# Pooled and banded attention in front of two layers of products: wider fillers, a mask and a sum given to TensorE, and a new plan of the order

## The chip, the cores and the metric

The program runs on one core of one Trainium2 chip. The metric is the device time of one execution in microseconds (us), lower is better; the median over several executions is taken. Beside the times, one profiled execution is recorded, with every instruction of the engines: TensorE (PE, its weight loads apart as PEld), VectorE (DVE), ScalarE (ACT), GpSimd (POOL) and SyncE (SP), which issues nearly all transfers here.

## What is computed

```python
def _attn_ref(q, k, v):                       # B, H, S, D = 4, 8, 576, 64
    q_d, k_d, v_d = means of q, k, v over groups of 4 positions
    out_d = softmax(q_d k_d^T / 8) v_d
    out_up = np.repeat(out_d, 4, axis=2)
    mask = np.abs(pos[:, None] - pos[None, :]) < 4
    out_local = softmax(where(mask, q k^T / 8, -1e9)) v
    return out_up + out_local

def reference(**kwargs):
    x = attn_out.transpose(0, 2, 1, 3).reshape(2304, 512)
    h = x @ w_in;  g = h * sigmoid(h);        x = g @ w_out    # 512 -> 2048 -> 512
    h = x @ w2_in; g = s * relu(h) ** 2 + b;  return g @ w2_out
```

All of it is fp32. The kernel reaches that precision in the layers by splitting each operand into a high and a low part that TensorE takes at full rate (fp32r), and by three matmuls for each product: high times high, low times high, high times low. The products of the attention are plain fp32 matmuls; the trace shows each of these as two records.

## The kernel before, in words

The 2304 tokens are cut into five blocks of 512, 512, 512, 512 and 256 (`blocks`). `mix1(u)` is the first layer for block u: for each of the 16 pieces of the hidden width it makes `hp` (12 matmuls of 512 columns), SiLU on ScalarE (`g`), a high part on ScalarE (`gh`), a low part on VectorE (`gl`), and then 12 matmuls into the four sums `y`. The second layer is computed with fewer products by sums of its operands: `group` makes its hidden values in the banks `ha`, `hb`, `hc` (and `hp` for the last block), `snap` copies a bank to SBUF (the `COPY g<-ha` of L350), `late` does Relu on ScalarE, the square on VectorE and scale and bias on ScalarE, and the result is stored to HBM (`gd<-g`) and read back (`graw<-gd`) for the last products `oa`, `ob`, `oc`.

Block 0 needs the attention of the first batch, and nothing of a layer can start before it. This stretch, up to about 45 us, is made of eight *pieces*: `banded` is called for each pair of heads (four) and each half of the batch's first 512 positions. A piece scores (`pB`, L841), adds the mask of the band on VectorE (`be<-pB,band`, L846), takes the minimum (L867) and the exponentials (L854), turns the result (`pBT`, L882) and copies it (`bat`), multiplies by V (`pBO`, L895) and adds the pooled attention on VectorE (`xf<-pBO,upT`, L904). When all pieces of a head pair are there, `x_split(0)` makes the high part `xh` on ScalarE (L584) and the low part `xl` on VectorE (L585), each 128x512, four times. The rest of the attention is done between the matmuls of the first blocks.

The order is not written by hand. Each operation is given to a planner (`Weave.op`) with its engine, a cost in us, what it reads and writes, and a number `pr`; `Weave.plan` goes through time and always starts what can start first, the lower `pr` first, and `Weave.run` emits the program in that order. Operations marked `EITHER` go to ScalarE or VectorE as the plan finds them free. The tables at the top (`P_...`, `NAT0`, `PB0`, ...) give these numbers and so the order on every engine and in the queue of SP. Where the plan leaves PE idle by over 0.12 us before block 0's split is done, `Weave.run` puts fillers in: matmuls on zeros into a bank that is not read (`spin`), as many of 64 columns as 0.85 of the planned gap holds at 0.03 us each. 100 fillers stand at the program's start (`NWARM`).

The second layer's weights come as 64-bit integers of fp64 bits and are converted once (`whole`, 32 times; `to_f32`): with `ACTW2` a ScalarE operation (L400, `f<-w_raw`) and two on VectorE (L403 and L410), without it three on VectorE (L408, L410, L412). What is converted is stored, and `y_sums`, `w_sums` and `out_sums` later load it again as `wt`, `wb` and `wout`; a `CAST wt<-wt` on ScalarE follows each load of `wt`.

Of the kernel before, what the change touches and what calls it, by code (L numbers as in the profile page):

```python
# [42 lines left out]
NNAT, NVW = 10, 4  # L43
AHEAD = 4
MORE = 0.0
RAW, KEEP = 1.68, 0.82
NEARLY = 0
MASKED = False
ADDED = False
P_IN, P_OUT, P_Y0, P_W0, P_Y1, P_Y4, P_W, P_OS = 163.074, 237.937, 134.047, 31.694, 78.573, -4.134, 81.417, 4.352  # L50
P_STEP, P_BT, P_PO, P_PN = 6.074, -5.7, 16.567, 57.528
P_G, P_B, P_C = 89.387, -1.232, -7.24
D1, D1S = 8, 2
NWARM = 100
ACTW, ACTW2 = 0, True
TANH = 0
# [9 lines left out]

NAT0, NATS = -3.387, 1.422
VW0, VWS, VW1 = 6.355, 0.281, 27.579
RAWF, RAW0, RATE = 35.769, 5.781, 1.255
DECF, DEC0, DECS = 47.826, 49.984, 0.829  # L70
PT0, PTS = 31.757, 3.611
PN0, PNS = 5.815, 6.313
PB0, PBS = -2.568, 16.345
NAT1, PT1, PT1S = 33.957, 58.357, 3.543
LDP = 49.468

# [209 lines left out]
def pe(n):  # L286
    return n / 2400.0 + 0.0145


@with_exitstack  # L290
def kernel(ctx, tc, q, k, v, w1_in, w1_out, w2_in, w2_out, s2, b2, cst, out):
# [82 lines left out]
    op("sp", (1, 0.25), lambda: dma(csb.tile, cst[:, :P]), w=[csb], pr=-100)  # L374
    op("sp", (1, 0.3), lambda: dma(band.tile, cst[:, P + 2 * NM:]), w=[band], pr=-2.9)
    by_chunk = cst[:, P:P + 2 * NM].rearrange("(k c) m -> c k m", k=KD)
# [4 lines left out]
    pad = fixed(cp, [P, 24], F32, "pad")  # L381
    idle = Buf("g", [P, P], BF16, "idle")
    spin = Buf("y3", [P, 64], F32, "spin")
    op("dve", 0.1, lambda: nc.vector.memset(idle[:], 0.0), w=[idle], pr=-200)

    def fill(n):
        for _ in range(n):
            nc.tensor.matmul(spin[:], lhsT=idle[:], rhs=idle[:, :64], start=True, stop=True)

# [36 lines left out]
    def weights(m, pr, after, lpr=None):  # L426
        got = []
        end = mark("end")
        for nm in ("wi", "wo"):
            t = Buf("w", [P, KD, P, 2], I32, nm + "_raw")  # L430

            op("sp", (1, 1.45 if nm == "wi" else 1.27), lambda t=t, nm=nm: load_in(w1_in, m, t[:]) if nm == "wi" else load_out(w1_out, m, t[:]),
               w=[t], r=after, pr=pr if lpr is None else lpr)
            f = Buf("f32", [P, KD, P], I32, "f32")
            o = Buf("w", [P, 2, KD, P], F32R, nm)
            to_f32(t, f, pr, [end], 0.0, m >= ACTW, m < GPS)
            halves(f, o, pr)
            got.append(o)
# [172 lines left out]
    def rows(b, i, names, pr, kind, after=[], by="sp"):  # L611

        for nm in names:
# [10 lines left out]

            op(by, (2, 1.35, 0.45) if nm == "v" else (2, 1.45, 0.5), load, w=[t], r=after, pr=pr)

# [155 lines left out]
    def b_load(b, hqs, js, pr, after=[]):  # L782
# [21 lines left out]
        k = (2 if mid else 0) + len(ends)  # L804
        move = 0.188 * len(js) * len(hqs)
        op(by, (k, move, 0.5), load, w=[vw], r=after, pr=pr)
        return vw

    def banded(b, hqs, js, vw, vi, pr, ps, after=[]):
# [97 lines left out]
        if added:  # L907
            (xh, xl), (e, i), cols = [t[hqs[0] // 2] for t in xs[u]], divmod(hqs[0], 2), slice(col, col + n)
            key = (hqs[0], js[0])
            op(EITHER, (act(n), dve(n)), lambda eng: copy(eng, xh[:, i, cols], pO[:]), w=[(xh, key)], r=[pO], pr=-4)  # L910
            op("dve", dve(n), lambda: nc.vector.tensor_tensor(out=xl[:, i, cols], in0=pO[:], in1=xh[:, i, cols].bitcast(F32), op=ALU.subtract),
               w=[(xl, key), (split[u][0], key)], r=[pO, (xh, key)], pr=-4)
        else:
            op("dve", dve(nb * QB), add, w=keys, r=[pO] + ups, pr=pr)
# [61 lines left out]
    for hq in A:  # L976
        rows(0, hq, "qk", NAT0 + NATS * hq, "nat")
        rows(0, hq, "v", NAT0 + NATS * hq, "nat", by="act" if hq < NACT else "sp")
    vw0 = [v_load(0, [hq], first, VW0 + VWS * hq) for hq in A]
# [443 lines left out]
```

## Time and profile before

| | us |
|---|---|
| median of 3 executions | 861.76 (861.71 to 862.54) |
| the profiled execution | 864.08 |
| its span, first to last instruction | 862.3 |
| PE busy in the span | 852.2 (99%) |
| VectorE busy | 735.2 (85%) |
| ScalarE busy | 509.0 (59%) |
| mean granted clock of TensorE | 0.998 |

The span is the execution without 1.8 us around it. The busy times are shares of the whole span and hide that the engines' loads differ from stretch to stretch; a busy PE includes the fillers. Matmuls overlap, so the time from the start of one to the start of the next tells what one costs, not its own length.

### The profile page before, as it was taken

The page shows a single profiled execution, that of the slowest core. Times are in us where ns is not written, and L with a number is a line of the kernel's source. Part 1 is how long each engine was busy: PE and PEld are TensorE (multiplying, and loading weights), DVE is VectorE, ACT ScalarE, POOL GpSimd, SP SyncE. Part 2 cuts the span into 40 slices and gives each one's busy share as a digit, 9 for nine tenths or more (in the row PEclk, how much of TensorE's full clock was granted, in tenths as well). Part 3 has the DMA queues.
Part 4 walks back from the last instruction along what each step waited for, and adds up shares of the span by engine and source line. Part 5 has one row for each costly group of instructions (what it writes and reads, how often), then busy time and mean ns, then how long its engine had stood idle before and what let it go on. Part 6 is the DMA issues. An engine that isn't in the chain of part 4 may idle for free. (4 is left out here: it accounts for less than half of the span.)

```text
span 862.3 us, 14707 instructions
## 1 busy us (share of the span) xinstructions
PE 852.2 (99%) x5300; PEld 715.3 (83%) x5300; DVE 735.2 (85%) x1364; ACT 509.0 (59%) x1034; POOL 0.2 (0%) x4
## 2 busy tenths in 40 slices
PE   9999999999999999999999999999998999999998
PEld 8878777778778878888889988888887888888887
DVE  7999996999999999987767789777775899888894
ACT  6988797655456742453556556666666665434351
POOL 0000000000000000000000000000000000000000
PEclk9999999999999999999999999999999999999999
DMA  8995421642444220489995246655577856544411
GB/s 204 297 379 157 129 69 40 195 125 70 106 127 118 70 75 32 128 278 304 335 307 162 75 130 218 219 183 178 181 255 246 271 170 211 173 148 129 122 32 43
DMA packets 163058, 144.26 MB, mean 167 GB/s; under 512 B 65452, under 2 KB 127786, under 8 KB 162986
## 3 DMA queue, kind: packets, MB, share of 16 engines
q1 hardware_dynamic: 162578, 142.96, 52.8%
q8 instruction: 42, 0.69, 0.3%
q10 hardware_dynamic: 408, 0.36, 0.1%
q14 instruction: 30, 0.25, 0.1%
HBM read 102.40 MB, written 40.89 MB: 166 GB/s over the span
## 5 line engine op out<-in xcount | busy, mean ns | idle before, releaser
L925 PE MATMUL hp<-xh,wi 128*128 128x512 f32 (+1 forms) x640 | 200.8, 377 | 0.2 <-ACT g L950 0.2
L925 PE MATMUL y<-gh,wo 128*128 128x512 f32 (+1 forms) x640 | 199.8, 376 | 0.0
L925 PEld LDWEIGHTS hp<-xh,wi 128*128 128x128 f32 x640 | 116.9, 188 | 23.1 <-ACT g L950 2.7
L925 PEld LDWEIGHTS y<-gh,wo 128*128 128x128 f32 x640 | 117.0, 189 | 19.9 <-issue 0.8
L925 PE MATMUL y<-gl,wo 128*128 128x512 f32 (+1 forms) x320 | 118.2, 369 | 0.0
L925 PE MATMUL hp<-xl,wi 128*128 128x512 f32 (+1 forms) x320 | 117.9, 369 | 0.0
L925 PE MATMUL ha<-yh,wi 128*128 128x512 f32 x256 | 87.8, 393 | 2.4 <-ACT g L350 2.4
L951 ACT CAST gh<-g 128x512 fp32r<-128x512 f32 (+1 forms) x80 | 46.1, 577 | 53.3 <-PE y L925 52.6
L950 ACT ACTIVATE g<-hp 128x512 f32<-128x512 f32 (+1 forms) x80 | 44.4, 555 | 42.1 <-DVE gl L952 36.9
L1138 ACT ACTIVATE g<-g,sbt 128x512 f32<-128x512 f32 (+1 forms) x72 | 54.7, 766 | 23.5 <-DVE g L1133 23.0
L925 PEld LDWEIGHTS y<-gl,wo 128*128 128x128 f32 x320 | 60.5, 189 | 8.8 <-DVE gl L952 0.3
L925 PEld LDWEIGHTS hp<-xl,wi 128*128 128x128 f32 x320 | 60.5, 189 | 8.2
L952 DVE TENSOR_TENSOR gl<-g,gh 128x512 fp32r<-128x512 f32 (+1 forms) x80 | 50.6, 633 | 17.7 <-ACT gh L951 17.6
L1133 DVE SCALAR_TENSOR_TENSOR g<-g 128x512 f32<-128x512 f32 (+1 forms) x80 | 49.7, 633 | 13.7 <-ACT g L1132 13.2
L925 PEld LDWEIGHTS ha<-yh,wi 128*128 128x128 f32 x256 | 48.4, 189 | 13.2 <-ACT g L350 3.7
L1265 ACT CAST gh<-gs 128x1024 fp32r<-128x1024 f32 x27 | 28.4, 1051 | 44.8 <-DVE gs L1261 37.2
L1265 ACT CAST gh<-graw 128x1024 fp32r<-128x1024 f32 x36 | 37.4, 1050 | 24.6 <-PE ob L1291 9.7
L925 PE MATMUL ha<-yl,wi 128*128 128x512 f32 x128 | 50.2, 393 | 0.0
L1266 DVE TENSOR_TENSOR gl<-graw,gh 128x1024 fp32r<-128x1024 f32 x36 | 43.6, 1218 | 4.9 <-PE oa L1284 4.0
L350 ACT COPY g<-ha 128x512 f32<-128x512 f32 x48 | 28.1, 585 | 31.1 <-PE ha L925 25.1
L925 PE MATMUL hc<-yh,wi 128*128 128x512 f32 x128 | 45.4, 395 | 0.0
L542 DVE TENSOR_TENSOR tmp<-le,lv 128x1344 f32<-128x1344 f32 (+1 forms) x28 | 37.9, 1354 | 0.5
(198 smaller groups left out, 1723.0 us busy)
## 6 DMA issues: line engine op xcount, KB each, us to landing
graw<-gd SPq DMA_DIRECT2D x36, 512.0 KB
gd<-g SPq DMA_DIRECT2D x64, 256.0 KB
wi_raw<-in_moe_w_in_dram SPq DMA_DIRECT2D x16, 512.0 KB
wo_raw<-in_moe_w_out_dram SPq DMA_DIRECT2D x16, 512.0 KB
w_raw<-in_moe_w_in_dram SPq DMA_DIRECT2D x16, 512.0 KB
w_raw<-in_moe_w_out_dram SPq DMA_DIRECT2D x16, 512.0 KB
nq<-in_q_dram SPq DMA_DIRECT2D x32, 144.0 KB
nk<-in_k_dram SPq DMA_DIRECT2D x32, 144.0 KB
```

The source lines that it names most:

```text
L350: (nc.scalar.copy if eng == "act" else nc.vector.tensor_copy)(out=out, in_=in_)
L542: op("dve", dve(n * WIN * D), lambda t=t, i0=i0, n=n, h2=h2: nc.vector.tensor_tensor(out=t[:], in0=wide(e[:, h2 * ns + i0:h2 * ns + i0 + n ...
L925: nc.tensor.matmul(t(), lhsT=lhs(i), rhs=rhs(i), start=(first and i == 0), stop=(last and i == 2), **kw)
L950: op("act", act(n), lambda g=g, hp=hp: nc.scalar.activation(out=g[:], in_=hp[:], func=AF.Silu), w=[g], r=[hp], pr=-5, table="silu")
L951: op("act", act(n), lambda g=g, gh=gh: nc.scalar.copy(out=gh[:], in_=g[:]), w=[gh], r=[g], pr=-5)
L952: op("dve", dve(n), lambda g=g, gh=gh, gl=gl: nc.vector.tensor_tensor(out=gl[:], in0=g[:], in1=gh[:].bitcast(F32), op=ALU.subtract), w=[gl ...
L1133: op("dve", dve(n) + 1.5 * MORE, lambda: nc.vector.scalar_tensor_tensor(out=t[:], in0=t[:], scalar=0.0, in1=t[:], op0=ALU.max, op1=ALU.mul ...
L1138: nc.scalar.activation(out=t[:], in_=t[:], func=AF.Identity, scale=sbt[:, 0:1], bias=sbt[:, 1:2])
L1265: op("act", act(HF * P) + MORE, lambda: nc.scalar.copy(out=flat(hi), in_=flat(x)), w=[hi], r=[x], pr=pr + n)
L1266: op("dve", dve(HF * P) + MORE, lambda: nc.vector.tensor_tensor(out=flat(lo), in0=flat(x), in1=flat(hi).bitcast(F32), op=ALU.subtract), w= ...
```

## The change

Fillers: `fill` makes one filler of 256 columns of every four of 64; the 100 at the start stay. `MASKED`: in the eight pieces of the first batch the mask is added by TensorE, as a product of the identity and the band into the same bank (`pB<-band,csb`, L837 after); the VectorE addition is gone, and minimum and exponentials read the bank. `ADDED`: the pooled attention is added in the same way (`pBO<-upT,csb`, L892 after, one of 256 columns for each piece), and `xh` and `xl` are made from the bank, piece by piece, 128x256 each. `ACTW2` is off. `AHEAD` (how many pieces of the first layer's weights may be loaded ahead of their conversion) goes from 4 to 3. The planner's costs for a few loads change, among them the longer blocks of keys of V, and all tables of numbers are new. All lines below the table move down by one or two.

```diff
-AHEAD = 4
+AHEAD = 3
-MASKED = False
-ADDED = False
-P_IN, P_OUT, P_Y0, P_W0, P_Y1, P_Y4, P_W, P_OS = 163.074, 237.937, 134.047, 31.694, 78.573, -4.134, 81.417, 4.352
+MASKED = True
+ADDED = True
+P_IN, P_OUT, P_Y0, P_W0, P_Y1, P_Y4, P_W, P_OS = 122.797, 178.953, 66.766, 19.092, 141.386, -9.23, 157.685, 125.641
...
-ACTW, ACTW2 = 0, True
+ACTW, ACTW2 = 0, False
...
-    return n / 2400.0 + 0.0145
+    return n / 2400.0 + 0.0143
...
-    idle = Buf("g", [P, P], BF16, "idle")
-    spin = Buf("y3", [P, 64], F32, "spin")
+    idle = Buf("g", [P, 4 * 64], BF16, "idle")
+    spin = Buf("y3", [P, 4 * 64], F32, "spin")
...
     def fill(n):
-        for _ in range(n):
-            nc.tensor.matmul(spin[:], lhsT=idle[:], rhs=idle[:, :64], start=True, stop=True)
+        wide, n = divmod(n, 4) if n < NWARM else (0, n)
+        for k in [4] * wide + [1] * n:
+            nc.tensor.matmul(spin[:, :64 * k], lhsT=idle[:, :P], rhs=idle[:, :64 * k], start=True, stop=True)
...
-            op(by, (2, 1.35, 0.45) if nm == "v" else (2, 1.45, 0.5), load, w=[t], r=after, pr=pr)
+            op(by, (2, 1.15, 0.45) if nm == "v" else (2, 1.27, 0.5), load, w=[t], r=after, pr=pr)
...
-        move = 0.188 * len(js) * len(hqs)
+        move = (0.25 if b == 0 and len(hqs) == 1 else 0.188) * len(js) * len(hqs)
...
-            (xh, xl), (e, i), cols = [t[hqs[0] // 2] for t in xs[u]], divmod(hqs[0], 2), slice(col, col + n)
+            (xh, xl), half, cols = [t[hqs[0] // 2] for t in xs[u]], hqs[0] % 2, slice(col, col + n)
...
-    for hq in A:
-        rows(0, hq, "qk", NAT0 + NATS * hq, "nat")
-        rows(0, hq, "v", NAT0 + NATS * hq, "nat", by="act" if hq < NACT else "sp")
+    for hq in A:
+        for nm in "qkv":
+            rows(0, hq, nm, NAT0 + NATS * hq + (PV if nm == "v" else 0.0), "nat", by="act" if nm == "v" and hq < NACT else "sp")
```

What `MASKED` and `ADDED` switch stands in `banded`, `x_split` and `parts` above, in the branches on `early` and `added`.

**First place.** PE at the first score of the first batch: `spin` are fillers, `pq` turns q and k of a head pair, `pB` is a piece's bank. Before:

```order
L388 LDWEIGHTS idle
L388 MATMUL spin<-idle 128x64
L841 MATMUL pB<-qkT 64x72 x16
L702 MATMUL pS<-dk,q_diag_87 96x144 x3
L774 MATMUL pq<-csb,nq 128x96 x6
```

After:

```order
L837 MATMUL pB<-band,csb 128x72
L837 MATMUL pB<-band,csb 128x216
L843 MATMUL pB<-qkT 64x72 x8
L837 MATMUL pB<-band,csb 128x288
L843 MATMUL pB<-qkT 64x72 x8
L704 MATMUL pS<-dk,q_diag_87 96x144 x3
L776 MATMUL pq<-csb,nq 128x96 x3
L776 MATMUL pq<-csb,nk 128x96 x6
L776 MATMUL pq<-csb,nq 128x96 x3
L390 LDWEIGHTS idle
L390 MATMUL spin<-idle 128x256
```

The two pieces of a head pair, 16 scores in one row before, stand together in both. The first now begins with two products of the mask (72 and 216 columns) and the second with one (288 columns); the fillers are cut into pieces of 256 columns. Over the whole program the order of PE has 368 fillers before; after, 100 at the start, 15 of 256 columns and 9 of 64. The new products are 12 of the mask and 8 of the pooled sum. The times that PE goes from other work into the layers' products are 92 before and 88 after.

**Second place.** ScalarE ahead of the copy for which PE waits near 662 us, a copy of bank `ha` (`g_7582` before, `g_7348` after), from the last cast of `wt`. Before:

```order
L350 CAST wt_7457<-wt_7457 128x512
L1132 ACTIVATE g_7502<-ha 128x512
L1138 ACTIVATE g_7484<-g_7484,sbt 128x256
L1132 ACTIVATE g_7528<-hp_7504 128x256
L1138 ACTIVATE g_7502<-g_7502,sbt 128x512
L1138 ACTIVATE g_7443<-g_7443,sbt 128x512
L1138 ACTIVATE g_7528<-g_7528,sbt 128x256
L1132 ACTIVATE g_7553<-hp_7524 128x256
L1138 ACTIVATE g_7553<-g_7553,sbt 128x256
L1132 ACTIVATE g_7568<-hp_7544 128x256
L1138 ACTIVATE g_7568<-g_7568,sbt 128x256
L350 COPY g_7582<-ha 128x512
```

After:

```order
L351 CAST wt_7223<-wt_7223 128x512
L1134 ACTIVATE g_7275<-hp_7225 128x256
L1140 ACTIVATE g_7253<-g_7253,sbt 128x512
L1134 ACTIVATE g_7293<-hp_7267 128x256
L1140 ACTIVATE g_7275<-g_7275,sbt 128x256
L1134 ACTIVATE g_7311<-hp_7287 128x256
L1140 ACTIVATE g_7205<-g_7205,sbt 128x512
L1140 ACTIVATE g_7293<-g_7293,sbt 128x256
L1140 ACTIVATE g_7311<-g_7311,sbt 128x256
L1134 ACTIVATE g_7334<-hp_7307 128x256
L1140 ACTIVATE g_7334<-g_7334,sbt 128x256
L351 COPY g_7348<-ha 128x512
```

Ten operations stand between the last cast and the copy in both, three of 512 columns before and two after. Before, the last four are Relu (L1132), scale (L1138), Relu, scale, each scale directly behind its own Relu, with the square of the same values on VectorE (L1133) between them; after, only the last pair stands so.

**Third place.** The queue of SP that feeds these casts: `wt` are the loads, `gd<-g` stores of hidden values, `w2t` stores of sums. Before:

```order
L363 DMA wt_7387<-w2t_92 128x512
L363 DMA wt_7394<-w2t_92 128x512
L363 DMA gd_95<-g_7367 128x512
L363 DMA wt_7419<-w2t_92 128x512
L363 DMA wt_7422<-w2t_92 128x512
L363 DMA gd_94<-g_7398 128x512
L363 DMA wt_7436<-w2t_92 128x512
L363 DMA wt_7445<-w2t_92 128x512
L363 DMA wt_7457<-w2t_92 128x512
L363 DMA gd_95<-g_7338 128x512
L363 DMA gd_94<-g_7380 128x512
```

After:

```order
L364 DMA wt_7153<-w2t_92 128x512
L364 DMA wt_7158<-w2t_92 128x512
L364 DMA w2t_93<-f_7027 128x512
L364 DMA gd_95<-g_7137 128x512
L364 DMA gd_94<-g_7165 128x512
L364 DMA wt_7188<-w2t_92 128x512
L364 DMA wt_7192<-w2t_92 128x512
L364 DMA gd_95<-g_7109 128x512
L364 DMA wt_7212<-w2t_92 128x512
L364 DMA wt_7217<-w2t_92 128x512
L364 DMA wt_7223<-w2t_92 128x512
L364 DMA gd_94<-g_7151 128x512
```

The eighth load of `wt`, an early one, is not among these rows. Before, the last three loads have the store of `gd_94<-g_7398` ahead of them and that of `gd_95<-g_7338` behind; after, both stores (`gd_94<-g_7165` and `gd_95<-g_7109`) are ahead of the last three loads, and the first of them ahead of the two loads before these as well.

**Fourth place.** VectorE at the start of the conversion of the second layer's weights (`w_raw`). Before:

```order
L567 TENSOR_TENSOR xf<-pt,upT 128x4x32 x2
L550 TENSOR_TENSOR tmp<-tmp 128x2x192
L952 TENSOR_TENSOR gl<-g,gh 128x512
L550 TENSOR_TENSOR tmp<-tmp 128x2x128
L403 TENSOR_SCALAR f_4540<-f_4540 128x512
L550 TENSOR_TENSOR pv<-tmp 128x2x64
L410 SCALAR_TENSOR_TENSOR f_4540<-w_raw,f_4540 128x512
L403 TENSOR_SCALAR f_4564<-f_4564 128x512
L403 TENSOR_SCALAR f_4578<-f_4578 128x512
L410 SCALAR_TENSOR_TENSOR f_4564<-w_raw,f_4564 128x512
L410 SCALAR_TENSOR_TENSOR f_4578<-w_raw,f_4578 128x512
```

After:

```order
L410 SCALAR_TENSOR_TENSOR f_4280<-w_raw,f_4280 128x512
L412 SCALAR_TENSOR_TENSOR f_4280<-w_raw,f_4280 128x512
L408 TENSOR_SCALAR f_4300<-w_raw 128x512
L410 SCALAR_TENSOR_TENSOR f_4300<-w_raw,f_4300 128x512
L408 TENSOR_SCALAR f_4311<-w_raw 128x512
L412 SCALAR_TENSOR_TENSOR f_4300<-w_raw,f_4300 128x512
L410 SCALAR_TENSOR_TENSOR f_4311<-w_raw,f_4311 128x512
L412 SCALAR_TENSOR_TENSOR f_4311<-w_raw,f_4311 128x512
L408 TENSOR_SCALAR f_4329<-w_raw 128x512
```

The operation that reads `w_raw` first was on ScalarE and is now L408 on VectorE, directly ahead of the other two or between those of the next conversion. Both orders have 32 conversions.

## Rows read from the trace of the kernel before

**Rows 1.** Busy time by stretch: us, each engine (instructions), clock, DMA share, GB/s; sum.

```profile
5.80:45.00 39.20, 38.23 (x700) 33.17 (x698) 37.88 (x113) 35.06 (x138) 0.00 (x0) 1.00 0.91 269
...
300.00:640.00 340.00, 340.00 (x1761) 290.58 (x1760) 271.31 (x508) 187.20 (x336) 0.00 (x0) 1.00 0.57 188
...
660.00:670.00 10.00, 8.00 (x28) 6.10 (x27) 3.73 (x6) 4.81 (x8) 0.00 (x0) 0.83 0.96 303
...
sum 862.30, PE 852.21 PEld 715.26 DVE 735.23 ACT 508.97 POOL 0.20; mean PE 106.53 PEld 89.41 DVE 91.90 ACT 63.62 POOL 0.03
```

**Rows 2.** Waits of PE: releaser, us in total, times, longest.

```profile
PE ha L925 <- ACT g L350: 2.4, 2, 2.0
...
PE pBO L895 <- ACT gh L951: 0.8, 1, 0.8
```

**Rows 3.** Groups of PE to 60 us: count, busy us, mean ns, idle before.

```profile
L388 PE MATMUL spin<-idle 128*128 128x64 bf16 x368 | 15.2, 203 | 1.0 <-DVE idle L384 1.0
```

**Rows 4.** Timeline of PE from 28 us: start, us, instruction.

```profile
29.04 2.19 PE L388 MATMUL spin<-idle 128*128 128x64 bf16 x69
31.06 0.88 PE L725 MATMUL pT<-csb,de 96*72 96x96 f32 x6
...
31.87 0.95 PE L702 MATMUL pS<-dk,q_diag 128*96 128x144 f32 x6
32.56 0.48 PE L925 MATMUL hp<-xh,wi 128*128 128x512 f32 x1
32.88 0.39 PE L925 MATMUL hp<-xl,wi 128*128 128x512 f32 x1
33.11 0.40 PE L925 MATMUL hp<-xh,wi 128*128 128x512 f32 x1
33.44 0.35 PE L741 MATMUL pU<-dat,nv 72*64 72x144 f32 x2
```

**Rows 5.** Groups of VectorE to 60 us, columns as in rows 3.

```profile
L846 DVE TENSOR_TENSOR be<-pB,band 128x288 f32<-128x288 f32 (+2 forms) x13 | 4.1, 353 | 0.0
...
L904 DVE TENSOR_TENSOR xf<-pBO,upT 128x256 f32<-128x256 f32 x8 | 3.1, 413 | 0.0
...
L585 DVE TENSOR_TENSOR xl<-xf,xh 128x512 fp32r<-128x512 f32 x4 | 2.7, 680 | 0.0
```

**Rows 6.** Timeline of ScalarE from 650 us, columns as in rows 4.

```profile
653.75 0.62 ACT L350 CAST wt<-wt 128x512 fp32r<-128x512 f32 x1 [2.25 <-DMA wt<-w2t]
...
654.99 0.60 ACT L350 CAST wt<-wt 128x512 fp32r<-128x512 f32 x1
...
657.56 2.02 ACT L1138 ACTIVATE g<-g,sbt 128x512 f32<-128x512 f32 x3 [0.71 <-DVE g L1133]
...
661.69 0.60 ACT L1138 ACTIVATE g<-g,sbt 128x256 f32<-128x256 f32 x1 [0.49 <-DVE g L1133]
662.20 0.56 ACT L350 COPY g<-ha 128x512 f32<-128x512 f32 x1
```

**Rows 7.** Timeline of PE from 659.5 us.

```profile
660.43 0.39 PE L925 MATMUL hb<-yh,wi 128*128 128x512 f32 x1
662.82 0.50 PE L925 MATMUL ha<-yh,wi 128*128 128x512 f32 x1 [2.00 <-ACT g L350]
...
667.27 0.40 PE L925 MATMUL ha<-yh,wi 128*128 128x512 f32 x1
```

**Rows 8.** Busy time by stretch around the weight loads, columns as in rows 1.

```profile
645.00:650.00 5.00, 4.56 (x23) 3.67 (x22) 4.18 (x8) 4.33 (x7) 0.00 (x0) 1.00 0.88 250
```

**Rows 9.** Groups of the second layer's weight conversion, 100 to 640 us.

```profile
L410 DVE SCALAR_TENSOR_TENSOR f<-w_raw,f 128x512 int32<-128x512 int32 x32 | 22.0, 690 | 0.7
L400 ACT ACTIVATE f<-w_raw 128x512 f32<-128x512 f32 x32 | 21.0, 668 | 13.9 <-DMA w_raw<-in_moe_w_in_dram 9.7 <-DMA w_raw<-in_moe_w_out_dram 2.2 <-DMA w2in<-f 1.0
...
L403 DVE TENSOR_SCALAR f<-f 128x512 int32<-128x512 int32 x38 | 15.9, 422 | 12.3 <-ACT f L400 12.2
```

**Rows 10.** VectorE busy in the stretch of most of these conversions.

```profile
365.00:450.00 85.00, 62.98 (x130) 1.00 0.89 303
```

More of the change, by code (lines that the diff above doesn't have):

```diff
@@ L47 @@
 NEARLY = 0
-MASKED = False
-ADDED = False
-P_IN, P_OUT, P_Y0, P_W0, P_Y1, P_Y4, P_W, P_OS = 163.074, 237.937, 134.047, 31.694, 78.573, -4.134, 81.417, 4.352
-P_STEP, P_BT, P_PO, P_PN = 6.074, -5.7, 16.567, 57.528
-P_G, P_B, P_C = 89.387, -1.232, -7.24
-D1, D1S = 8, 2
+MASKED = True
+ADDED = True
+P_IN, P_OUT, P_Y0, P_W0, P_Y1, P_Y4, P_W, P_OS = 122.797, 178.953, 66.766, 19.092, 141.386, -9.23, 157.685, 125.641
+P_STEP, P_BT, P_PO, P_PN = 4.73, 9.579, 17.31, 56.675
+P_G, P_B, P_C = 228.726, -47.225, -4.311
+D1, D1S = 7, 2
 NWARM = 100
-ACTW, ACTW2 = 0, True
+ACTW, ACTW2 = 0, False
 TANH = 0
@@ L64 @@
 FAR = float(2 ** 33)
[L67 to L75, printed above, removed]
+NAT0, NATS = -7.342, 2.644
+VW0, VWS, VW1 = -1.608, 2.538, 8.932
+RAWF, RAW0, RATE = 21.534, 1.046, 2.892
+DECF, DEC0, DECS = 52.571, 49.3, 1.001
+PT0, PTS = 8.069, 1.782
+PN0, PNS = -7.062, 4.844
+PB0, PBS = -25.963, 23.549
+NAT1, PT1, PT1S = 36.887, 62.603, 1.163
+LDP = 53.052
+PBD, PV = -38.666, 1.948
 class Slot:
@@ L374 @@
     op("sp", (1, 0.25), lambda: dma(csb.tile, cst[:, :P]), w=[csb], pr=-100)
-    op("sp", (1, 0.3), lambda: dma(band.tile, cst[:, P + 2 * NM:]), w=[band], pr=-2.9)
+    op("sp", (1, 0.3), lambda: dma(band.tile, cst[:, P + 2 * NM:]), w=[band], pr=PBD)
     by_chunk = cst[:, P:P + 2 * NM].rearrange("(k c) m -> c k m", k=KD)
@@ L430, in weights @@
             t = Buf("w", [P, KD, P, 2], I32, nm + "_raw")
-            op("sp", (1, 1.45 if nm == "wi" else 1.27), lambda t=t, nm=nm: load_in(w1_in, m, t[:]) if nm == "wi" else load_out(w1_out, m, t[:]),
+            op("sp", (1, 1.33 if nm == "wi" else 1.3), lambda t=t, nm=nm: load_in(w1_in, m, t[:]) if nm == "wi" else load_out(w1_out, m, t[:]),
                w=[t], r=after, pr=pr if lpr is None else lpr)
@@ L907, in banded @@
         if added:
-            (xh, xl), (e, i), cols = [t[hqs[0] // 2] for t in xs[u]], divmod(hqs[0], 2), slice(col, col + n)
+            (xh, xl), half, cols = [t[hqs[0] // 2] for t in xs[u]], hqs[0] % 2, slice(col, col + n)
             key = (hqs[0], js[0])
-            op(EITHER, (act(n), dve(n)), lambda eng: copy(eng, xh[:, i, cols], pO[:]), w=[(xh, key)], r=[pO], pr=-4)
-            op("dve", dve(n), lambda: nc.vector.tensor_tensor(out=xl[:, i, cols], in0=pO[:], in1=xh[:, i, cols].bitcast(F32), op=ALU.subtract),
+            op(EITHER, (act(n), dve(n)), lambda eng: copy(eng, xh[:, half, cols], pO[:]), w=[(xh, key)], r=[pO], pr=-4)
+            op("dve", dve(n), lambda: nc.vector.tensor_tensor(out=xl[:, half, cols], in0=pO[:], in1=xh[:, half, cols].bitcast(F32), op=ALU.subtract),
                w=[(xl, key), (split[u][0], key)], r=[pO, (xh, key)], pr=-4)
```

## The prediction

> **What bounds the kernel now.** I read the busy times by stretch first. PE has 340.00 of 340 us between 300 and 640 us and 852.21 of 862.30 over the span [rows 1], so all that it does lies on the path: a matmul added costs its pitch, and time can be won only where PE waits, idles or runs fillers. The waits of PE name little: the longest is one of 2.0 us for a copy by ScalarE [rows 2]. The rest is filler time, ahead of the layers. In the front, from 5.8 to 45 us, PE is busy for 38.23 of 39.2 us, but VectorE too, for 37.88 us, and ScalarE for 35.06 us [rows 1]. So VectorE paces that stretch, and PE bridges it with 268 of the 368 fillers (100 belong to the start) [rows 3].
>
> **The first batch's mask and sum.** VectorE loses 12 mask additions at 353 ns and 8 sums at 413 ns (one mask of the 13 in the group is a later piece's) and four subtractions at 680 ns [rows 5], 4.2 + 3.3 + 2.7 = 10.2 us. Eight subtractions of 256 columns come in their place, of the size of the sum's 413 ns, 3.3 us. That takes 6.9 us from VectorE in the stretch that it paces. PE gains the work: 12 mask products with 4 x (72 + 216 + 288) = 2304 columns and 8 of 256, 2048 columns. No such product is in the trace; the nearest is the plain fp32 score of 144 columns, where six records take 32.56 - 31.87 = 0.69 us [rows 4], or 0.80 ns for each column of a record. At two records for each matmul the mask costs 2304 x 2 x 0.80 = 3.7 us and the sum 3.3 us, +7.0 us together. Below this the columns cannot go, since no faster fp32 form stands in the rows; above, a weight load that isn't hidden would add for each of the 40 records some 0.05 us (the entry into a product after other work costs 0.09, below), +9 us. I take 7.0, as these have a full array and long rows like the scores.
>
> **The fillers.** 69 fillers of 64 columns take 31.06 - 29.04 = 2.02 us, 29.3 ns each [rows 4]. 268 of them are 7.85 us. The order after has 15 of 256 columns, at four times the price 117 ns, and 9 of 64: 2.0 us. That is -5.85 us. A filler stands for a gap in the plan and covers 0.85 of it, so with each 0.85 us of filler goes 0.15 us of idle PE: 7.85 x 15/85 = 1.4 us before, 0.35 us after, -1.0 us. What hides the products is therefore time in which PE had nothing but fillers: +7.0 - 5.85 - 1.0 = +0.15 us. That VectorE is 6.9 us shorter and PE's fillers as much fewer says the same from the other side: the front turns from a stretch paced by VectorE into one in which PE, VectorE and ScalarE are all close to full, and it does not get shorter. Small waits have less cover there: I add +0.5 us, for the size of the one that is there now, 0.8 us for a high part [rows 2]; the bounds are 0 and 2 us.
>
> A wide filler by itself is no gain: four of 64 fill the same time.
>
> **The turns.** The first layer product after other work starts its successor 32.88 - 32.56 = 0.32 us later, the next 0.23; the last before other work holds it off for 33.44 - 33.11 = 0.33 us [rows 4]. A turn away and back so costs about 0.2 us. Four fewer of them: -0.8 us.
>
> **The wait near 662 us.** PE starts its last matmul into `hb` at 660.43 and the next, into `ha`, at 662.82 us: 2.39 us where the pitch is 0.23, 2.16 us lost [rows 7]. Behind it, the clock falls: the stretch 660 to 670 has a mean granted clock of 0.83 [rows 1], and the next 12 matmuls take 667.27 - 662.82 = 4.45 us [rows 7] instead of 12 x 0.23 = 2.7, another 1.7 us. The place costs 3.9 us. PE goes on 0.62 us after the copy of ScalarE starts, at 662.20 us [rows 6], so the copy would have to start at 660.04 us.
>
> What makes it late stands on ScalarE. The cast of a weight waits 2.25 us for its load, until 653.75 us; the last cast starts at 654.99, the copy 7.2 us later [rows 6]. In these 7.2 us the scales wait for the squares on VectorE: 0.71 us once, and 0.49 us twice, in the two pairs Relu, scale right ahead of the copy (the second is shown) [rows 6]. The order after keeps one of these pairs and spreads the others, so 0.71 + 0.49 us go, and one operation of 512 columns becomes one of 256, about 0.2 us: 5.8 us from cast to copy. The casts also follow one another with no scale between the last two, so the last may start up to 0.5 us earlier. Against this, the last loads come behind one more store of 256 KB, 1.05 us at the 250 GB/s of that time [rows 8], if the queue is as full as before. The copy then starts between 654.5 + 5.8 = 660.3 and 655.0 + 5.8 + 1.05 = 661.85 us, 0.3 to 1.8 us late. I take 1.0 us, the middle, with the clock up since the engine rests half as long: from 3.9 to 1.0, **-2.9 us**. The bounds are 0 and -3.9 us.
>
> A rule of the Trainium skill speaks against this step. "DMA: Bandwidth & Descriptors", section "Queues, rings and completion order", says that each DMA engine takes the descriptors of one ring in their order, so a load issued behind a store starts behind it. By that the later end of the span just given holds, 1.8 us late, and with the fallen clock the sum would be 2.9 us higher; no row here shows two transfers apart.
>
> **The conversions.** Without the ScalarE operation (668 ns, 32 times, 21.0 us) VectorE has one more, like that at 690 ns: 32 x 0.69 = +22 us [rows 9]. Most lies between 365 and 450 us, where VectorE is busy for 62.98 of 85 us [rows 10]: 22 us are free. So the stretch is just filled. What hides it is that PE has no wait in the whole of 300 to 640 us [rows 1] though VectorE waited there 12.2 us in the conversion itself [rows 9]: the low parts are ready microseconds ahead of their matmuls. I cost it at nothing; without that cover up to 22 + 12.2 - 22 = 12 us.
>
> The new tables and load costs change only the order; where they move nothing that PE waits for they cost nothing, since PE has no other idle time to lose or win, and what they do at the places above is counted there. The load ahead (4 to 3) is hidden by the same cover; without it, a late weight would stop PE for a load.
>
> **The sum.** +0.15 + 0.5 - 0.8 - 2.9 = -3.05 us. Against the span, 862.3, this gives 859.2; the profiled execution, 1.8 us longer than its span, would be 861.0. The median of the runs, 861.76, is 2.3 us below that execution, and I apply the change to it: 861.76 - 3.05 = 858.7 us. Own range, with the wait near 662 winning from 1.8 to 3.9 and the small waits at 0 to 1 us: 857.2 to 860.3.
>
> **The rivals.** *The wait stays.* The last weight lands a store later, the copy is 1.8 us late or more and the clock falls as before: nothing won but the turns, 0.15 + 0.5 - 0.8 = -0.15, 861.6 us. For it speaks the order of SP's queue, against it that ScalarE's chain is shorter. It gets about half the forecast's chance, since the span of the copy's start, 660.3 to 661.85 us, reaches its late end only with a full queue and no earlier cast. (By the skill's rule of the ring's order it would get more.)
>
> *VectorE becomes the bound at the conversions.* The three operations of a conversion stand in one queue with the low parts, and its first one waits for the load of the raw weight (ScalarE waited 9.7 + 2.2 us there [rows 9]). In order, each low part behind them is late, and PE waits for it. Up to 3 us of price it only eats the gain; above 3.05 + 1.7 = 4.8 us of the 12 it makes the kernel slower. Halfway, at 6 us, 864.8 us.
>
> *The front gains too.* If VectorE alone set the end of the front, and the products fit into time in which PE is idle beside fillers, all 6.9 us of VectorE could show up to what idle and filler allow; with all of the 3.9 us at 662 and half of the front, -3.9 - 0.8 - 2 = -6.7, 855.1 us. Against it: PE's own work is the same as the time won.
>
> *The change does not take the load off*: the products cost 9 us, their weight loads not hidden, and the rest goes as in the sum: 858.7 + 2 = 860.7 us, inside the range.
>
> **Chances.** Forecast 0.47, the wait stays 0.25, VectorE bounds the conversions 0.18 (a quarter of it with a price that only cancels the gain), the front gains 0.10. 0.2% is 1.7 us, about what a measurement of this kernel tells from no change. Faster: 0.47 less a little for the upper end of its range, and 0.10, 0.56. Slower: 0.18 less the cancelling quarter, and a little of the wait that stays with more small waits, 0.17. Within: 0.27. The range leaves out about 0.1 at each end: 855.2 to 863.4 us.
>
> **What the profile after would show.** Right: some 2 us of fillers after the start, products of the mask at 0.8 ns a column of a record, no mask addition or sum of the first batch on VectorE and still no wait of PE above 1 us before 60 us, the copy wait near 660 under 1.2 us at clock 1.00, and no wait of PE for `gl` between 360 and 460. Wrong: a wait of 2 us and a clock under 1.00 there (second case), PE waiting for VectorE between 365 and 490 (third), or waits of several us before the first product of the first layer.

## The result and the profile after

The change made the kernel slower: 867.02 us (median of 5 executions, 865.84 to 868.95) against 862.07 us (861.71 to 864.11) on the same chip, a ratio of 1.0054 with a 95% interval from 1.0038 to 1.0069, or some 4.6 us. The forecast was 858.7 us. The profiled execution after has a span of 865.3 us, 3.0 us more than the span shown before. In a second profile of the kernel before (below) the span is 859.2 us; against that one it is 6.1 us more.

The busy time by stretch after, columns as in rows 1; it answers to [rows 1]:

```profile
5.80:45.00 39.20, 37.78 (x454) 29.84 (x450) 33.64 (x100) 31.91 (x134) 0.00 (x0) 1.00 0.95 277
...
300.00:640.00 340.00, 339.48 (x1768) 288.87 (x1767) 285.08 (x536) 170.96 (x314) 0.00 (x0) 1.00 0.55 183
640.00:660.00 20.00, 18.45 (x84) 14.66 (x83) 15.42 (x32) 13.12 (x27) 0.00 (x0) 1.00 0.84 291
660.00:670.00 10.00, 10.00 (x64) 8.84 (x63) 6.96 (x13) 7.75 (x16) 0.00 (x0) 1.00 0.63 196
...
sum 865.30, PE 855.52 PEld 714.01 DVE 747.00 ACT 483.46 POOL 0.20; mean PE 106.94 PEld 89.25 DVE 93.38 ACT 60.43 POOL 0.03
```

VectorE has 33.64 us in these 39.2 us, where it had 37.88. PE has 37.78 us there, nearly what it had, though almost all its fillers are gone: the new products have taken their place. In 660 to 670 us PE is busy throughout at full clock; the fall to 0.83 is not there. PE's total is 3.3 us up.

Where the front ends is told by the first product into `y`. Ahead of it PE has the same 480 records in both kernels, beside the fillers and the new products. Its start in the second profile of the kernel before, and after:

```profile
53.45 0.39 PE L925 MATMUL y<-gh,wo 128*128 128x512 f32 x1
```

```profile
58.39 0.39 PE L927 MATMUL y<-gh,wo 128*128 128x512 f32 x1
```

The front is 4.9 us longer (in the first profile of before this product starts at 53.55 us). So the loss lies there; of the 6.1 us between the two spans only 1.2 us fall behind it.

The waits of PE after, which answer to [rows 2], and those of VectorE up to 60 us:

```profile
PE ha L927 <- ACT g L351: 1.6, 2, 0.8
...
PE pq L776 <- DMA nq<-in_q_dram: 1.0, 1, 1.0
```

```profile
DVE bst L869 <- PE pB L843: 2.9, 4, 2.0
```

No new wait of PE is above 1.0 us. The new one that matters is VectorE's: the minimum (`bst`, L869) waits 2.9 us for PE's scores, 2.0 us at once. In the front VectorE now waits for PE.

What the new products cost is read from PE's timeline, from start to start. The scores and the products with V use 64x64 or 72x64 of TensorE's array (64*64 in a row below) and are called narrow here; the products of the mask and the sum use all of it, 128x128. A change between the two is a turn. The first pair of pieces, its mask and scores, and a later pair's pooled sum and products with V, after:

```profile
9.29 0.78 PE L837 MATMUL pB<-band,csb 128*128 128x72 f32 x4
10.00 0.72 PE L843 MATMUL pB<-qkT 64*64 64x72 f32 x16
10.65 0.75 PE L837 MATMUL pB<-band,csb 128*128 128x288 f32 x2
11.33 0.72 PE L843 MATMUL pB<-qkT 64*64 64x72 f32 x16
11.98 0.98 PE L704 MATMUL pS<-dk,q_diag 128*96 128x144 f32 x6
```

```profile
31.22 0.59 PE L892 MATMUL pBO<-upT,csb 128*128 128x256 f32 x2
31.74 0.69 PE L897 MATMUL pBO<-bat,vw 72*64 72x64 f32 x16
32.36 0.70 PE L892 MATMUL pBO<-upT,csb 128*128 128x256 f32 x2
32.99 0.69 PE L897 MATMUL pBO<-bat,vw 72*64 72x64 f32 x16
33.60 0.63 PE L884 MATMUL pBT<-csb,be 128*72 128x128 f32 x4
```

The pair of scores with its masks takes 11.98 - 9.29 = 2.69 us, and the pair with the pooled sum 33.60 - 31.22 = 2.38 us. Before, 32 records of such scores took 8.70 - 7.52 = 1.18 us (second profile), and 32 of the products with V 29.04 - 27.95 = 1.09 us (first profile, the end in [rows 4]):

```profile
7.52 1.23 PE L841 MATMUL pB<-qkT 64*64 64x72 f32 x32
8.70 0.95 PE L702 MATMUL pS<-dk,q_diag 128*96 128x144 f32 x6
```

```profile
27.95 1.15 PE L895 MATMUL pBO<-bat,vw 72*64 72x64 f32 x32
```

That is 1.51 us for the mask of a pair and 1.29 us for its sum. In the third pair the two pieces' scores stand apart in both kernels, and its masks take 0.68 + 0.61 = 1.29 us. Over the four pairs the mask costs 5.8 us and the sum 5.2: **11.0 us**, where the forecast has 7.0.

### The profile page after: what moved, and what is told of

Its sections match the earlier page's. It is cut to its first block, busy times and chain, and to the rows that moved or that the text cites. A ratio compares the mean times of both kernels' runs of the same rounds, so it can differ in the third digit from the quotient of the medians.

```text
span 865.3 us, 14210 instructions
## 1 busy us (share of the span) xinstructions
PE 855.5 (99%) x5096; PEld 714.0 (83%) x5096; DVE 747.0 (86%) x1373; ACT 483.5 (56%) x1010; POOL 0.2 (0%) x4
## 5 line engine op out<-in xcount | busy, mean ns | idle before, releaser
L927 PE MATMUL y<-gh,wo 128*128 128x512 f32 (+1 forms) x640 | 197.7, 374 | 0.0
L952 ACT ACTIVATE g<-hp 128x512 f32<-128x512 f32 (+1 forms) x80 | 44.4, 555 | 49.4 <-DVE gl L954 39.2
L1140 ACT ACTIVATE g<-g,sbt 128x512 f32<-128x512 f32 (+1 forms) x69 | 52.2, 763 | 24.8 <-DVE g L1135 24.4
```

The source lines that it names most:

```text
L927: nc.tensor.matmul(t(), lhsT=lhs(i), rhs=rhs(i), start=(first and i == 0), stop=(last and i == 2), **kw)
L952: op("act", act(n), lambda g=g, hp=hp: nc.scalar.activation(out=g[:], in_=hp[:], func=AF.Silu), w=[g], r=[hp], pr=-5, table="silu")
L1140: nc.scalar.activation(out=t[:], in_=t[:], func=AF.Identity, scale=sbt[:, 0:1], bias=sbt[:, 1:2])
```

## The experiments

A ratio is that of a kernel's runs to those of the kernel before on the same chip, with its 95% interval; 0.001 is 0.86 us. *After* is at 1.0054 [1.0038, 1.0069]. Changing a cost or an operation makes the planner set a new order for the whole program, so the first group keeps the order of the kernel after row for row and changes only what PE is given there. Beside the times, the start of the first product into `y` tells what a run of this group does to the front (58.39 us after); a span also holds what a single execution wins or loses behind it.

### The products, in the order of the kernel after

**Left out.** The loops of the products are skipped, and the matmuls behind them start their banks themselves:

```diff
-            if early:
+            if False:
                 for k, (w0, i0, i1) in enumerate(spans):
...
-                if added:
+                if False:
                     p0 = js[c0] * QB // 4
```

> The kernel after in its own order, with the 12 mask products and the 8 products of the pooled sum left out of PE (so the mask and the pooled attention of the first batch's first 512 positions are missing from the output); nothing comes back on VectorE. Theory A: the products cost 10 us of PE time on the path, not 7, because each stands between narrow matmuls (64x64) and pays a turn into and out of the full array beside its columns: 10 us faster than the kernel after, less some 1 to 2 us of PE idle that then shows, 858 to 859 us. Rival B: PE is not what sets the front's end after the change; VectorE or ScalarE do, and PE only idles where the products were: under 3 us faster, 864 or more. Rival C: the loss lies behind 60 us, in the new order: also under 7 us faster.

Measured: 863.0 us, 1.0015 [1.0005, 1.0026]. By the ratios 3.4 us are won of the 11.0, just more than B allows and far from A's 10. The front agrees:

```profile
55.41 0.39 PE L927 MATMUL y<-gh,wo 128*128 128x512 f32 x1
```

That is 3.0 us earlier than in the kernel after. The spans differ by 6.0 (859.3 us), but this execution is 1.9 us under the median of its kernel, and some 2 us of the 6.0 fall at the copies near 645 us, where PE waits in the profile after (below) and not here. The rest of the 11.0 comes back as PE that stands idle:

```profile
5.80:45.00 39.20, 33.70 (x448) 26.10 (x445) 34.98 (x103) 32.85 (x138) 0.00 (x0) 1.00 0.96 285
```

PE idles 5.5 of 39.2 us there, 1.4 after. So a next bound stands some 3 us behind PE in this order. And without any product, with all that VectorE was relieved of, the kernel is still slower than before, by 0.4 to 2.2 us, and its front 2.0 us longer.

**Turns.** The second piece of a pair gets its full-array products behind its narrow ones, so that the order mask, scores, mask, scores becomes mask, scores, scores, mask; the same for the pooled sum:

```diff
+        behind = early and js[0] > 0
...
         def score():
-            if early:
+            if early and not behind:
+                masks()
...
+            if behind:
+                masks()
```

> The kernel after with the same operations and the same order, but in the second piece of each pair of heads the mask product and the pooled product stand behind that piece's narrow matmuls and not ahead, so that the narrow matmuls of both pieces stand together: two turns between full and narrow array fewer for each of 4 + 4 pairs, 16 turns. Theory A (turns of about 0.1 us each, and a weight load that is hidden): 1.5 to 2.3 us faster, 865 us, and the first record behind a narrow matmul no longer 0.1 us longer. Rival D (the columns of the products are slow themselves, through their broadcast operands, and turns cost nothing): no change within 0.5 us, 867 us.

Measured: 865.05 us, 1.0048 [1.0032, 1.0065]. The times don't tell it from the kernel after. The trace does, for the same two pairs:

```profile
9.60 0.78 PE L838 MATMUL pB<-band,csb 128*128 128x72 f32 x4
10.31 1.23 PE L848 MATMUL pB<-qkT 64*64 64x72 f32 x32
11.47 0.75 PE L838 MATMUL pB<-band,csb 128*128 128x288 f32 x2
12.06 0.90 PE L704 MATMUL pS<-dk,q_diag 128*96 128x144 f32 x6
```

```profile
30.85 0.59 PE L901 MATMUL pBO<-upT,csb 128*128 128x256 f32 x2
...
32.99 1.11 PE L891 MATMUL pBT<-csb,be 128*72 128x128 f32 x8
```

2.46 us for 2.69, and 2.14 for 2.38, with the same records: two turns fewer save 0.23 and 0.24 us, so a turn between the narrow and the full array costs 0.12 us. The masks of the third pair, whose scores stand apart, gain nothing. The first product into `y` starts at 56.94 us, 1.45 us earlier. The span is 1.9 us shorter (863.4), but 1.2 us of that come at the copies near 645 us; ahead of them the lead is down to 0.7. Theory A's part on turns holds in the trace; whether the columns are slow besides (D) is read from the mask issued twice, below.

**The mask in bf16.** Identity and band are cast once to bf16 on GpSimd, which is idle:

```diff
+    op("pool", 0.3, lambda: nc.gpsimd.tensor_copy(out=idle[:, 4 * 64:4 * 64 + P], in_=csb.tile), w=[identb], r=[csb, idle], pr=-30)
+    op("pool", 0.3, lambda: nc.gpsimd.tensor_copy(out=idle[:, 4 * 64 + P:], in_=band.tile), w=[bandb], r=[band, idle], pr=-30)
...
-                    nc.tensor.matmul(pB[:, i0:i1], lhsT=ident, rhs=band[:, w0:w0 + KW].unsqueeze(1).to_broadcast([P, i1 - i0, KW]),
+                    nc.tensor.matmul(pB[:, i0:i1], lhsT=idle[:, 4 * 64:4 * 64 + P], rhs=idle[:, 4 * 64 + P + w0:4 * 64 + P + w0 + KW].unsqueeze(1).to_broadcast([P, i1 - i0, KW]),
```

> The kernel after with the same order, the identity and the band cast once to bf16 by GpSimd (both are exact there), so that each mask product is one record in place of two and a column takes a quarter of the time; the turns stay. Theory A: the mask products fall from 5.4 us in the trace to about 12 x 0.1 plus 2304 columns x 0.44 ns = 2.0 to 2.5 us, 3 us faster, 864 us. Rival B or C: under 1.5 us faster.

Measured: 863.72 us, 1.0032 [1.0021, 1.0044], 1.9 us faster than the kernel after by the ratios and 4.1 by the spans (861.2). The masks of a pair, 0.71 + 0.68 us in the kernel after, take 0.22 + 0.23:

```profile
9.04 0.29 PE L840 MATMUL pB<-idle 128*128 128x72 bf16 x2
9.26 0.72 PE L846 MATMUL pB<-qkT 64*64 64x72 f32 x16
9.92 0.30 PE L840 MATMUL pB<-idle 128*128 128x288 bf16 x1
10.15 0.72 PE L846 MATMUL pB<-qkT 64*64 64x72 f32 x16
```

Four pairs save 3.7 us of PE. The first product into `y` starts at 55.73 us, 2.7 us earlier; the rest of the 4.1 is made behind the front, at the copies near 645 us.

**Both cures together.** The last two edits in one kernel, in the same order.

> The kernel after in its own order with both cures: mask products in bf16, and the products of the second piece behind its narrow matmuls. Theory A: the sum of the two that ran alone (about 3 and 1 us faster than the kernel after), 863 us, still at or above the kernel before, since the pooled products and the order remain. If it is below 861 us, the order after is better than that of before once the products are cheap.

Measured: 863.15 us, 1.0017 [1.0005, 1.0029], 3.2 us faster than the kernel after, as expected, and still above the kernel before. The first product into `y` starts at 55.22 us, where it starts with no products at all (55.41). So with some 5 us off the products' 11.0 the next bound is reached, and taking off the rest wins nothing more.

**The mask twice.** Each mask product is issued a second time over the first:

```diff
-                for k, (w0, i0, i1) in enumerate(spans):
+                for k, (w0, i0, i1) in [*enumerate(spans)] * 2:
```

> The kernel after in its own order with the mask products issued twice (the second time over the first, so the result is the same): 5.4 us more of PE time at the trace's price, no more turns, nothing else. Theory A (PE sets the front's end in the kernel after): 5 us slower than it, 871.5 us. Rival B (others set it and PE has room): under 2 us slower. Leaving all products out won 3.4 us of 11.3; if adding costs its full price, PE is the bound in the change as it stands, and what came back as idle time when they left is where the next bound lies.

Measured: 870.7 us, 1.0095 [1.0069, 1.0121], 3.5 us slower than the kernel after by the ratios, 4.2 by the spans (869.5 to 865.3). The price of 5.4 us that the expectation took holds the turns of the first copies too, which the second don't pay. The trace has the price of the second copies alone, here for the first pair:

```profile
10.00 1.37 PE L837 MATMUL pB<-band,csb 128*128 128x72 f32 x8
11.30 0.72 PE L843 MATMUL pB<-qkT 64*64 64x72 f32 x16
11.95 1.24 PE L837 MATMUL pB<-band,csb 128*128 128x288 f32 x4
13.11 0.72 PE L843 MATMUL pB<-qkT 64*64 64x72 f32 x16
```

1.30 us for 0.71 and 1.16 for 0.68; over the four pairs the second copies add 4.3 us. The first product into `y` starts at 63.37 us, 5.0 us later, of which 0.7 were lost before the first mask (10.00 us for 9.29). It speaks for A: what is added to PE shows whole in the front.

### The kernel before

**Wide fillers alone.** The edit of `fill` and its two tiles, as in the change.

> The kernel before with only its fillers cut into 256 columns, in its own order. All theories: no change, 862 us within 0.5 us, since four fillers of 64 columns take what one of 256 takes. If wide fillers change the clock or keep PE from its real work longer, it shows here: 1 us or more either way. Also of interest: whether the wait and the lower clock near 662 us, seen in the profiled execution of the kernel before, are there again.

Measured: 862.29 us, 1.0004 [0.9993, 1.0015]. Wide fillers change nothing that the times show. The profiled execution has its first product into `y` at 55.01 us, 1.6 us later than the kernel before; the times' interval ends at 1.3 us, so this is not put down to the fillers. Around 660 us the clock is 1.00 in it, and no wait for a copy is above 0.4 us.

**Profiled again**, without an edit.

> The kernel before, profiled a second time. If the wait of 2 us and the lower clock near 662 us, on which 2.9 us of the forecast rested, belong to the kernel, they are here again: clock 0.83 in the stretch 660 to 670 us and 4.45 us for the 12 matmuls after the wait. If they belong to that one execution (theory E), the clock is 1.00 there, the wait under 1 us, the span near 860 us and under that of the first profile by about 2 us, as the times say: 861.6 us for the median, 864.1 for the execution profiled first.

Measured: 861.92 us, 0.9997 [0.9983, 1.0012], span 859.2 us. Theory E holds. Around 660 us, columns as in rows 1 and rows 4:

```profile
660.00:670.00 10.00, 9.05 (x40) 7.48 (x41) 5.07 (x7) 6.33 (x10) 0.00 (x0) 1.00 1.04 307
```

```profile
659.58 0.39 PE L925 MATMUL hb<-yh,wi 128*128 128x512 f32 x1
660.95 0.50 PE L925 MATMUL ha<-yh,wi 128*128 128x512 f32 x1 [0.98 <-ACT g L350]
...
663.82 0.39 PE L925 MATMUL ha<-yh,wi 128*128 128x512 f32 x1
```

The wait is 0.98 us, 660.95 - 659.58 - 0.23 = 1.14 us are lost, and the 12 matmuls behind take 663.82 - 660.95 = 2.87 us, not 4.45. The place costs 1.3 us, not the 3.9 of [rows 7]. The load that ScalarE waits for there is done earlier:

```profile
651.10 0.62 ACT L350 CAST wt<-wt 128x512 fp32r<-128x512 f32 x1 [1.33 <-DMA wt<-w2t]
...
660.33 0.56 ACT L350 COPY g<-ha 128x512 f32<-128x512 f32 x1
```

651.10 us where it was 653.75 [rows 6]. The place makes up 2.6 of the 3.1 us between the two spans. Why the load came so late in the execution profiled first, and whether that execution or its chip made it so, is open; the medians of the kernel before in the experiments are all between 861.6 and 862.3 us.

**The copy first.** The last Relu, square and scale ahead of the copy are put behind it (3133 to 3135 are their numbers in the plan, 3139 is the copy's); two rows of ScalarE change places with the copy and nothing else moves:

```diff
+        order = [i for i in order if i not in (3133, 3134, 3135)]
+        at = order.index(3139) + 1
+        order[at:at] = [3133, 3134, 3135]
```

> The kernel before with one move on ScalarE: the copy of bank ha, for which PE waits near 661 us, stands ahead of the last Relu and scale, not behind them; nothing else moves. It is what the forecast hoped the change would do there. Theory E (the place is worth what the second profile of before shows, a wait of 0.98 and 1.14 us lost, with no fall of the clock): 1.0 to 1.2 us faster than before, 860.8 us, at the edge of what can be told. If the first profile is typical (3.9 us): 3 us or more faster, under 859 us.

Measured: 861.53 us, 0.9999 [0.9987, 1.0011]. In the profile PE has no wait there any more:

```profile
640.00:660.00 20.00, 19.88 (x109) 16.89 (x108) 16.42 (x31) 16.04 (x31) 0.00 (x0) 1.00 0.81 276
660.00:670.00 10.00, 10.00 (x46) 8.29 (x45) 5.30 (x8) 6.28 (x11) 0.00 (x0) 1.00 0.94 273
```

From the product into `hp` that starts at 655.01 us in the second profile of before, and at 656.45 here, to the one into `ha` at 664.73, and 664.86 here, it gains 1.3 us. The times don't show this (it is as wide as the interval), and they rule out the 3 us.

### Parts of the change in orders of their own

These kernels are planned anew, so each shows its part and its order together.

**The mask alone and the sum alone**, each with the numbers of the kernel before, one of these two lines and wide fillers:

```diff
-MASKED = False
+MASKED = True
...
-ADDED = False
+ADDED = True
```

> The kernel before with its own numbers and wide fillers, and of the change the mask products alone; the planner then sets a new order from the old numbers, in which 4.9 us of fillers stand after the start instead of 7.8. Theory A (products at the price seen in the profile after, on PE's path): 5.4 us of products and 8 turns of 0.11 us, less 2.9 us of fillers and 0.5 us of unfilled gaps, 2.9 us slower than before, 864.5 us. Rival B (VectorE sets the front's end, and 4.2 us less on it shortens it): 1 us or more faster than before.

> The kernel before with its own numbers and wide fillers, and of the change the pooled sum by products alone; in its new order 5.6 us of fillers stand after the start. Theory A: 4.6 us of products and 8 turns of 0.11 us, less 2.2 us of fillers and 0.4 us of gaps, 2.9 us slower than before, 864.5 us. Rival B (VectorE, 2.7 us less on it): 0.5 us or more faster than before.

Measured: the mask alone 865.46 us, 1.0049 [1.0031, 1.0066]; the sum alone 868.78 us, 1.0084 [1.0066, 1.0102]. Both are slower than before, so B's gain does not come. The mask costs 4.2 us for 2.9 expected, the sum 7.2 for 2.9: more than the products, and the waits of PE for the sum alone name an order that is late elsewhere:

```profile
PE y L927 <- DVE gl L954: 3.3, 2, 2.0
```

**The mask in bf16 alone**, on the kernel before with `MASKED = True`, wide fillers, both cures above, and its cost told to the planner (the part of the line that changes):

```diff
-(0.12 * nb if early else 0)
+(0.05 * nb if early else 0)
```

> As the mask alone on the kernel before, but the mask products in bf16, with those of a pair's second piece behind its scores, and the planner told 0.05 us for a position in place of 0.12; 6.6 us of fillers stand after the start. Theory A: some 1.8 us of products and few turns, less 1.2 us of fillers and 0.2 of gaps: 0 to 1 us slower than before, so no gain, since PE's own work is what the front is made of. Rival B: 1 us or more faster.

Measured: 863.9 us, 1.0040 [1.0023, 1.0058], 3.4 us slower by the ratio and 2.0 by the medians where 0 to 1 was expected. In the profiled execution PE waits 2.9 us at one place for a copy on VectorE; that execution took 869.44 us, 5.5 above the median, so the wait need not be in the others:

```profile
PE pU L746 <- DVE dat L351: 2.9, 1, 2.9
```

**The conversions back on ScalarE**, in the kernel after; the order of PE is the same up to some 385 us and differs in a few hundred rows behind:

```diff
-ACTW, ACTW2 = 0, False
+ACTW, ACTW2 = 0, True
```

> The kernel after with the second layer's weights converted with ScalarE again, as before the change; its order differs little. Rival F (the conversions on VectorE are a part of the loss, by filling VectorE between 365 and 450 us): 2 us or more faster than the kernel after. Theory A: within 1 us of it, 866 us, since PE waits for nothing there in the profile after.

Measured: 866.26 us, 1.0046 [1.0031, 1.0061], 0.7 us faster than the kernel after, well inside the two intervals, with the same span (865.3 us). Nothing speaks for rival F.

**Both cures, and the planner told**, with the numbers of the kernel after; and **the mask in bf16 with the sum back on VectorE**, which has both cures too, the first line of costs and `ADDED = False` (of the lines of costs, the parts that change):

```diff
-(0.12 * nb if early else 0)
+(0.05 * nb if early else 0)
...
-(0.125 + 0.115 * added)
+(0.125 + 0.10 * added)
...
-ADDED = True
+ADDED = False
```

> The kernel after with both cures, and the planner told smaller costs for the products, so that it sets another order with the same numbers. If only the products' price matters: as with both cures in the order after, 863 us within 1 us. If the order from untuned numbers brings waits of its own, as the mask and the sum alone on the kernel before suggest: 1 to 5 us slower than that.

> The kernel after with the mask in bf16 products and the pooled sum back on VectorE, in the order that the planner sets then. Theory A on products alone: 4.3 us of pooled products less than with both cures, 2 to 3 us more fillers: 861 to 862 us. With waits from an untuned order: 864 to 867 us.

Measured: 870.87 us, 1.0109 [1.0092, 1.0127], and 875.35 us, 1.0155 [1.0140, 1.0171]. Both are slower than either expectation allows. The first has less work on PE than the kernel after, as its twin in the order after shows, and is 4.7 us slower than it. In the second PE waits 5.1 us at one place for VectorE:

```profile
PE pt L562 <- DVE pv L555: 5.1, 1, 5.1
```

No version here is faster than the kernel before beyond its interval.

## Why the prediction was wrong

**The products (the step that failed first).** "I take 7.0, as these have a full array and long rows like the scores." They cost 11.0 us, 4.0 more, and above the upper bound of 9. A smaller part is the columns: the second copies of the mask, with no turn of their own, take 4.3 us for 4608 columns of records, 0.93 ns each where 0.80 was taken, which makes 1.1 us over the 8704 columns of all the products. What was left out is where the products stand: between narrow matmuls, so that PE turns from the narrow array to the full one and back for a single product. The forecast had a price of that kind in its own rows, 0.09 and 0.10 us at both ends of the first layer's products [rows 4], and used it for four fewer turns of the layer but not for the new turns of the attention, two in each run of scores or of products with V that is now broken up, 14 in seven such pairs. At 0.12 us these are 1.7 us; the other 1.2 us were not measured apart. The Trainium skill, page "TensorEngine Tiling (Array Packing)", section "Key Properties", says that a change of the tiling mode drains TensorE; it gives no price, and the 0.12 us of the turns experiment are in line with it.

**The wait near 662 us (the second).** The forecast goes "from 3.9 to 1.0, -2.9 us". The row was read rightly, but it was of one execution: 864.08 us, 2.3 us above the median to which the forecast then applied the whole gain. In the second profile the place costs 1.3 us. The mechanism (the order on ScalarE makes the copy late) was right: the copy set first removes the wait, and in the kernel after PE goes on at this copy from `hb` to `ha` within 0.25 us, without one. But there it waits for two earlier copies of `ha`:

```profile
643.41 0.39 PE L927 MATMUL hc<-yh,wi 128*128 128x512 f32 x1
644.64 0.50 PE L927 MATMUL ha<-yh,wi 128*128 128x512 f32 x1 [0.84 <-ACT g L351]
...
647.31 0.39 PE L927 MATMUL ha<-yh,wi 128*128 128x512 f32 x1
648.40 0.50 PE L927 MATMUL ha<-yh,wi 128*128 128x512 f32 x1 [0.71 <-ACT g L351]
```

At a pitch of 0.23 us 1.9 us are lost at these two, 0.6 us more than the place cost in the second profile of before. So nothing was won, and nothing could have been beyond some 1.3 us.

**The fillers and what they stood for.** The count held: two dozen fillers are left after the start, -5.85 us, and their width changes nothing that the times show. The -1.0 us for the unfilled rest of the gaps did not come: PE's idle time in 5.8 to 45 us went from 0.97 to 1.42 us. But the forecast books filler time as time that the products can have, and adds only 0.5 us for waits. With the products left out, and nothing in their place, the front is not shorter than before but 2.0 us longer, at 55.41 us. With both cures, some 6 us of products, it ends at 55.22 us. So in this order products at the forecast's price would not have kept the front at +0.15 us either; some 2 us would have stood.

**Where the relief of VectorE went.** Its operations are gone as forecast, and the front did not get shorter, first because PE was given 11.0 us for some 7 us of fillers and gaps, and VectorE now waits for PE. What sets the front's end if the products cost nothing is open: PE waits then for several engines and loads in turn, 1.5 us at most, in an order that was made for slower products. From 5.8 us to the first product into `y` the DMA engines are busy for 0.98 of the time there and in the kernel after, and for 0.94 in the second profile of before, so loads are one candidate; no run tested it. The orders planned anew brought losses of their own.

**The turns of the layers**, four fewer, and the small waits were not measured by themselves.

**The conversions** are as forecast: VectorE is busier by 14 us between 300 and 640 us, PE loses 0.5 us there, and putting them back on ScalarE changes nothing that the times can tell.

**The sum again.** The front is 4.9 us longer where +0.15 was forecast, and of these 4.8 us the runs give 3.0 to 3.4 to the products and leave 1.4 to 1.8 open. With +2.9 for the wait, -3.05 becomes +4.6 us, as the times say, if turns and small waits are as forecast. Where the forecast lets the copy be 1.8 us late with the fallen clock, its own terms give 1.8 + 1.7 = 3.5 us, so the sum would be 2.5 us higher and not 2.9.

**The rivals.** That the wait stays is right in that nothing was won there, but not in its mechanism: the copy's wait is gone, and the clock did not fall. VectorE as the bound of the conversions did not come. That the products cost more was a rival inside the range, with too low an upper bound.

## What to carry to other kernels

Price an added matmul with its neighbours: a full-array product put between narrow ones costs its columns and a turn on each side, and with the second product of a pair behind the narrow run half of the turns go. Filler time is not free time: what PE waits for may still be there when the fillers are gone. Before a wait that one profile shows is booked as a gain, see whether that execution's own time stands at the median; here it stood 2.3 us above it, and the place made up 2.6 us. The same holds for a span read after an experiment: a landmark behind the changed stretch, such as the first product into `y`, says what the edit did there. Where a planner sets the order, test a part with the order held fixed: the kernel with both cures, two of its planner's costs changed and nothing else, went from 863.15 to 870.87 us.

## What the runs showed of the hardware

A mask product of 288 columns takes 0.68 us from start to start with fp32 operands between narrow matmuls, and 0.23 us in bf16. A second copy of the mask, behind the first, takes 0.93 ns for a column of a record. A turn between 64x64 or 72x64 tiles and the full array costs 0.12 us, the mean of two turns.
